# Routing inside a stream of expert products: the count product moved behind the spreading products, and turns of x placed behind routing products

## The chip, the cores and the metric

The kernel runs on one core of a Trainium2 chip. The metric is the device time of one execution in microseconds (us), as the median of several runs. The profiler takes one execution apart: PE is TensorE (its matmuls), PEld its weight loads, DVE is VectorE, ACT is ScalarE, POOL is GpSimd, SP issues DMAs.

## The reference

The input is attention with pooled keys and values, then a mixture of eight experts, each of which takes exactly 576 of 4608 tokens:

```python
def _moe_ref(x, w_gate, w1, w2):
    cap = N // E
    logits = x @ w_gate
    order = np.argsort(-logits.flatten())
    for idx in order:
        tok, e = (int(idx) // E, int(idx) % E)
        if assigned[tok] >= 0 or counts[e] >= cap:
            continue
        assigned[tok] = e
        counts[e] += 1
    ...
    for e in range(E):
        mask = assigned == e
        h = np.maximum(x[mask] @ w1[e], 0.0)
        out[mask] = h @ w2[e]
```

x has 512 columns, w1 is 512 x 1024 and w2 1024 x 512 for each expert. x is the attention's output: batch 8, 8 heads of 64, 576 positions.

## The kernel before, in words

The first 150 us are the attention, which also stores x in DRAM (`xd`) and makes the gate's logits `lg`, 128 partitions x 36 tokens x 8 experts. Then the experts run, one after the other, in the order in which they fill up. Which expert fills next and with which tokens is found by eight routing phases (`Routing.phase`). Phase 0 runs alone; phase k+1 runs in small pieces between the products of expert k.

A phase searches the threshold in four rounds. In each, DVE compares all tokens with 32 thresholds (`cmp`, L610), PE counts (nine products, L653, or L615 in phase 0), DVE picks the diagonal (`diagc`, `cnt`), PE folds (L665), DVE compares with what each expert still needs (`g`, L672), PE spreads the result to all partitions (L679), and DVE takes the maximum `up` (L681), from which the next round's places `q` come. Then `close` makes the expert's number `eid`, the running places of its tokens (PE: L713, L714), a one-hot product that puts token numbers into rows (L733, nine products), and the spreading of these to all partitions (L747, eight products). DVE turns that into `rows` (L750), with which POOL gathers the tokens' x from DRAM (`gather`, L987, five DMAs). At last DVE counts each partition's chosen tokens by expert (`per`, L759, and `pc`, L762), PE adds these over the partitions (L765), and DVE takes the sum off `need` (`left`, L767). All routing products write the one bank `rt`.

An expert has two stages. Both split f32 numbers into a high and a low part and multiply three times. Stage 1 (`stage1`, L1043) makes h = relu(x w1): 96 products of 256 columns, then 96 of 320. Stage 2 (`products`, L1077) makes 96 products of 512 columns, four rows of 24, and for the last 64 tokens 16 products at L1082. Ahead of them x must be turned: `xt` takes one piece of 128 tokens (the fifth has 64), makes four transposes into a bank `tp` (L1019; there are two such banks), ACT copies the high part `xh` and DVE the low part `xl` (L1023), which frees the bank. The weights are split in pieces by ACT (`w1h`, `w2h`) and DVE (`w1l`, L999, `w2l`, L1008), and stage 1's result by ACT (`hh`) and DVE (`hl`, L1051).

The order of everything is written at build time by the function `experts`, which keeps a clock of its own, `now`. After each main product it calls `advance`, which adds the product's expected duration and calls `step` when the expected end (`ready`) of the last routing piece on DVE has passed. `step` takes the next piece of the routing generator; a yield of two numbers tells what DVE will need until the next product may follow, and in all. `turns` places the next turn when its gather should have landed and 1.4 us have passed since the last turn; `first` and `lows` hold routing back for weights and for `xl`. `later` puts an instruction on DVE off by a given time. A routing product is thus put into PE's row at the place where its operand should be ready; if DVE is late, PE stands, as each engine works its row in order.

Of the kernel before, what the change touches and what calls it, by code (L numbers as in the profile page):

```python
# [11 lines left out]
BF = mybir.dt.bfloat16  # L12
# [3 lines left out]
OP = mybir.AluOpType  # L16
# [393 lines left out]
class Routing:  # L410
# [187 lines left out]
    def search(self, shadow, spare):  # L598
# [88 lines left out]
        self.sel = wk.tile([128, NC], BF, name="sel")  # L687
        nc.vector.tensor_scalar(self.sel, q16, up, 1.0 + EDGE, op0=OP.subtract, op1=OP.is_gt)

    def close(self, k, last):  # L690

        nc, wk, NC, lg = self.nc, self.wk, self.NC, self.lg
# [46 lines left out]
        with nc.allow_low_precision(reason="one number up to 1152 and zeros"):  # L739
            nc.vector.tensor_reduce(cp[:, 0], own, axis=AX.X, op=OP.add)  # L740
        nc.vector.tensor_scalar(cp[:, 1], cp[:, 0], 0.0, self.qcol, op0=OP.is_gt, op1=OP.mult)
        yield 0.6, 0.6
        cpv = cp.rearrange("p v (j g) -> p v j g", g=4)
        ps = self.psum()
        for g in range(4):
            for v in range(2):
                nc.tensor.matmul(ps[:, :5], self.spread[:, 96 - 32 * g:224 - 32 * g], cpv[:, v, :, g],  # L747
                                 start=(g == v == 0), stop=(g == 3 and v == 1))
        rows = wk.tile([128, 5], I32, name="rows", bufs=3)
        nc.vector.tensor_scalar(rows, ps[:, :5], -1.0, 0.0, op0=OP.add, op1=OP.max)  # L750
        self.rows = rows
# [3 lines left out]
        self.halves = halves  # L755
        yield 0.0, 0.2, "rows"

        per = wk.tile([128, NC, 8], BF, name="per")
        nc.vector.tensor_tensor(per, self.oh, sel[:, :, None].to_broadcast([128, NC, 8]), op=OP.mult)  # L759
        pc = wk.tile([128, 8], BF, name="pc")  # L760
        with nc.allow_low_precision(reason="counts up to 36"):
            nc.vector.tensor_reduce(pc, per.rearrange("p c e -> p e c"), axis=AX.X, op=OP.add)  # L762
        yield 1.15, 1.15
        ps = self.psum()
        nc.tensor.matmul(ps[:, :8], self.ones, pc, start=True, stop=True)  # L765
        left = wk.tile([128, 8], F32, name="left")
        nc.vector.tensor_tensor(left, self.need, ps[:, :8], op=OP.subtract)  # L767

        mis = wk.tile([128, 1], F32, name="mis")
        nc.vector.tensor_reduce(mis, left, axis=AX.X, op=OP.min)  # L770
# [379 lines left out]
def experts(ctx, tc, g, R, xd, w1, w2, out, ident, cap, keep):  # L1150
# [10 lines left out]

    lows = 0

    now, dve, ready = 0.0, 0.0, 0.0

    def later(after, t, f):
# [9 lines left out]

    def step(e):

        nonlocal now, ready, dve
        p, crit, t, what = held.pop() if held else next(g, (None, 0.0, 0.0, None))  # L1180
        if p is None:
            return False
        if what == "id":

            if p > e or p and pieces[p - 1].l < 8:
                held.append((p, crit, t, what))
                return False
            X.load_1(R.eid, 0, 4 if p else 2)
            eids[p] = R.eid
        elif what == "rows":  # L1190
            if p and turned[p - 1] < 5:
# [12 lines left out]
    def advance(e, t):  # L1204

        nonlocal now
        now += t
        while True:
            if waiting and waiting[0][0] <= now:
                flush(len(waiting) - 1)  # L1210
            elif ready > now or first(e) or not step(e):
                break
# [4 lines left out]
    class Pieces:  # L1217
# [10 lines left out]
        def next(self, ahead=True):  # L1228
            nonlocal dve
            if self.h == self.l:  # L1230
                self.up()
            if ahead:
                self.up()
            self.low(self.e, self.l)
            self.l += 1
            dve = max(dve, now) + 0.7
# [33 lines left out]
        elif (e, t) == (0, 4):  # L1270
            later(1.0, 0.2, lambda: X.load_2(behind(1)))

    def turns(e, upto, t0):
# [35 lines left out]
    for e in range(8):  # L1309
# [128 lines left out]
```

## Time and profile before

| | us |
|---|---|
| median of 3 runs (lowest, highest) | 624.25 (623.96, 625.15) |
| the profiled execution's own time | 624.06 |
| its span, first to last instruction | 622.2 |
| PE busy | 597.3 (96%) |
| DVE busy | 396.9 (64%) |
| ACT busy | 238.3 (38%) |

A row of the timeline gives the start, the length, the engine, line and operation, out<-in, the shape, how many of them were merged, and in brackets the idle time ahead of the first and what ended it. Matmuls overlap in these rows, as the length includes the way through the array; what one costs is the distance from its start to the next start. A row of waits gives who waited for whom, the sum, the number and the longest. A row of windows gives the stretch and its length, then the busy time and number of instructions of PE, PEld, DVE, ACT and POOL, the granted TensorE clock, the share of the DMA engines and GB/s.

### The profile page before, as it was taken

The numbers are of one execution on the slowest core, as the hardware profiler recorded it, in microseconds if no ns is written. First come the engines' busy times: TensorE is split into PE (matmuls) and PEld (weight loads), VectorE is DVE, ScalarE is ACT, GpSimd is POOL, SyncE is SP. The second block draws the span as 40 slices with busy tenths as digits, with TensorE's granted clock in tenths as the row PEclk, the third lists the DMA queues.
The fourth block names the chain that finished last, engine by engine and source line by source line (L and its number), as shares of the span: only waits on it lengthen the run. The fifth ranks groups of instructions, "written<-read, shape, count | busy, mean of one in ns | idle before, by whom it ended". The sixth has DMA issues, their size and how long they took to land.

```text
span 622.2 us, 11468 instructions
## 1 busy us (share of the span) xinstructions
PE 597.3 (96%) x4327; PEld 518.6 (83%) x4327; DVE 396.9 (64%) x1159; ACT 238.3 (38%) x554; POOL 180.1 (29%) x221
## 2 busy tenths in 40 slices
PE   8999999985999999999999999999999999999994
PEld 5999999973797789869978987897799889879972
DVE  7687777887796778858863985496378237505300
ACT  7444444451361434413532451254245225515210
POOL 2999998000200500413012302130230113020021
PEclk9999999995999999999999999999999999999997
DMA  9999961222442544319103701630190055014010
GB/s 355 419 424 410 424 219 72 76 97 85 137 145 63 200 162 135 93 52 328 29 35 130 261 1 51 238 135 18 52 330 27 34 182 207 18 52 145 2 45 36
DMA packets 32609, 92.16 MB, mean 148 GB/s; under 512 B 3473, under 2 KB 3473, under 8 KB 29857
## 3 DMA queue, kind: packets, MB, share of 16 engines
q1 hardware_dynamic: 21296, 62.92, 27.0%
q0 software_dynamic: 5920, 18.95, 9.0%
q10 hardware_dynamic: 5328, 9.48, 4.0%
q8 instruction: 35, 0.57, 0.4%
q14 instruction: 30, 0.24, 0.1%
HBM read 72.46 MB, written 18.87 MB: 147 GB/s over the span
## 4 chain that ended last, share of the span: by engine, by line
PE 83%; issue 7%; DVE 4%; DMA 2%; ACT 1%; POOL 1%; another core or an unknown queue 0%; POOLq 0%; ACTq 0%
PE h L1043 30%; PE h L1077 25%; PE psa L269 8%; PE pss L227 6%; PE h L1082 4%; PE tp L1019 2%; PE pse L256 2%; PE rt L256 1%; PE rt L653 1%; PE rt L217 1%; PE rt L615 1%; DMA rawk<-in_k_dram 1%; DMA out_dram<-yt,rows 1%; PE rt L208 1%; DMA xg<-xd,rows 1%
## 5 line engine op out<-in xcount | busy, mean ns | idle before, releaser
L1057 POOL DMA_INDIRECT out_dram<-yt,rows x29 | 31.4, 1082 | 247.0 <-ACT yt L1091 246.6
L1077 PE MATMUL h<-w2h,hh 128*128 128x512 f32 x256 | 102.5, 400 | 0.3 <-PEq L1141 0.3
L1077 PE MATMUL h<-w2l,hh 128*128 128x512 f32 x256 | 101.9, 398 | 0.0
L1077 PE MATMUL h<-w2h,hl 128*128 128x512 f32 x256 | 101.0, 395 | 0.0
L1043 PE MATMUL h<-xh,w1l 128*128 128x320 f32 (+1 forms) x512 | 95.4, 301 | 0.0
L1048 ACT ACTIVATE hh<-h 128x320 fp32r<-128x320 f32 (+1 forms) x128 | 52.4, 410 | 108.6 <-PE h L1043 102.6
L1043 PE MATMUL h<-xl,w1h 128*128 128x320 f32 (+1 forms) x512 | 92.8, 300 | 0.0
L1043 PE MATMUL h<-xh,w1h 128*128 128x320 f32 (+1 forms) x512 | 91.8, 300 | 0.3 <-ACT xh L1021 0.3
L987 POOL DMA_INDIRECT xg<-xd,rows x40 | 42.3, 1056 | 131.8 <-DVE rows L750 48.6
L1043 PEld LDWEIGHTS h<-xh,w1h 128*128 128x128 f32 x512 | 75.3, 190 | 3.5 <-issue 2.7
L1043 PEld LDWEIGHTS h<-xh,w1l 128*128 128x128 f32 x512 | 77.2, 189 | 0.5
L1043 PEld LDWEIGHTS h<-xl,w1h 128*128 128x128 f32 x512 | 76.2, 190 | 0.0
L1023 DVE TENSOR_TENSOR xl<-tp,xh 128x512 fp32r<-128x512 f32 (+1 forms) x40 | 25.3, 633 | 70.8 <-ACT xh L1021 70.1
L1051 DVE SCALAR_TENSOR_TENSOR hl<-h,hh 128x320 fp32r<-128x320 f32 (+1 forms) x128 | 56.7, 451 | 20.9 <-ACT hr L1050 16.0
L1091 ACT ACTIVATE yt<-h 128x512 f32<-128x512 f32 x32 | 19.1, 598 | 127.5 <-PE h L1077 83.6
L269 PE MATMUL psa<-vblk,eT 128*128 128x146 f32 (+3 forms) x400 | 62.1, 302 | 0.0
L1077 PEld LDWEIGHTS h<-w2l,hh 128*128 128x128 f32 x256 | 48.2, 188 | 8.9
L1077 PEld LDWEIGHTS h<-w2h,hh 128*128 128x128 f32 x256 | 48.4, 189 | 8.6 <-issue 0.7
L1077 PEld LDWEIGHTS h<-w2h,hl 128*128 128x128 f32 x256 | 48.2, 188 | 8.5
L269 PEld LDWEIGHTS psa<-vblk,eT 128*128 128x128 f32 (+1 forms) x400 | 52.2, 180 | 1.7 <-issue 0.3
L999 DVE TENSOR_TENSOR w1l<-raw,w1h 128x512 fp32r<-128x512 f32 x64 | 41.9, 687 | 13.0 <-ACT w1h L995 13.0
L1008 DVE TENSOR_TENSOR w2l<-raw,w2h 128x512 fp32r<-128x512 f32 x64 | 43.2, 681 | 3.4 <-ACT w2h L1005 3.4
(216 smaller groups left out, 898.8 us busy)
## 6 DMA issues: line engine op xcount, KB each, us to landing
raw<-in_moe_w_dram SPq DMA_DIRECT2D x64, 512.0 KB, 6.5
xd<-xt ACTq DMA_DIRECT2D x36, 256.0 KB, 4.4
rawv<-in_v_dram SPq DMA_DIRECT2D x7, 1280.0 KB, 14.0
rawk<-in_k_dram SPq DMA_DIRECT2D x7, 1152.0 KB, 13.8
rawq<-in_q_dram SPq DMA_DIRECT2D x7, 1152.0 KB, 12.2
rawk<-in_k_dram SPq DMA_DIRECT2D x2, 576.0 KB, 4.6
rawv<-in_v_dram SPq DMA_DIRECT2D x1, 768.0 KB, 7.8
rawq<-in_q_dram SPq DMA_DIRECT2D x1, 640.0 KB, 8.9
```

Source lines behind the costliest of these rows:

```text
L227: nc.tensor.matmul(ps[cols, j // 2, 144 * (j % 2):144 * (j % 2) + 144], self.q_of(b, j, n, cols.stop - cols.start), self.kblk[b % 4][:, j] ...
L269: self.nc.tensor.matmul(o[h], self.eT[i][:, c, h], self.vblk[b % 4][:, self.BLOCKS[c]:self.BLOCKS[c + 1]], start=(c == cs[0]), stop=(c == ...
L987: nc.gpsimd.indirect_dma_start(out=self.xg[:n, t, :], out_offset=None, in_=self.xd, in_offset=bass.IndirectOffsetOnAxis(ap=rows[:n, t:t + ...
L999: self.nc.vector.tensor_tensor(l, raw, h.bitcast(F32), op=OP.subtract)
L1008: self.nc.vector.tensor_tensor(self.w2l[:, i], self.raw2[e][:, i], self.w2h[:, i].bitcast(F32), op=OP.subtract)
L1023: later(1.3, 0.65, lambda: nc.vector.tensor_tensor(xl, ps[:, :, :n], xh, op=OP.subtract))
L1043: nc.tensor.matmul(ps[:, :m], a[:, j, fs], b[:, j, o], start=(n == 0), stop=(n == 11))
L1048: nc.scalar.activation(hh[:, f, o], ps[:, :m], AF.Relu)
L1051: later(0.65, 0.4, lambda f=f, o=o, m=m, ps=ps: nc.vector.scalar_tensor_tensor(hl[:, f, o], ps[:, :m], 0.0, hh[:, f, o].bitcast(F32), op0= ...
L1057: st = nc.gpsimd.indirect_dma_start(out=rows, out_offset=bass.IndirectOffsetOnAxis(ap=idx, axis=0), in_=y, in_offset=None)
L1077: nc.tensor.matmul(ps, a[:, f, o], b[:, f], start=(f == 0 and k == 0), stop=(f == 7 and k == 2))
L1082: nc.tensor.matmul(ps[64 * a:64 * a + 64, :256], self.hr[:, f], self.raw2[e][:, f, 256 * a:256 * a + 256], start=(f == 0), stop=(f == 7))
```

## The change

Three things are done. First, in all phases but 0 the counts of a partition (`per`, `pc`) are made on DVE ahead of the spreading products, right behind `cp`, and the product that adds them over the partitions follows directly behind the eight spreading products, into columns 8 to 15 of the same bank. The planner is told that DVE needs 1.75 us there, not 0.6. Second, `step` notes with `fresh` that it has just put a routing product into PE's row, and `turns` places a turn only then, or when the routing has ended (`through`), or when the turn is overdue (`t < late`). In stage 1 `turns` is now called behind `advance`, so that the turn stands directly behind the product. Third, the earliest place of a turn in stage 1 of experts 1 to 7 is no longer fixed at the tenth product.

```diff
@@ close @@
         nc.vector.tensor_scalar(cp[:, 1], cp[:, 0], 0.0, self.qcol, op0=OP.is_gt, op1=OP.mult)
-        yield 0.6, 0.6
+        if k:
+            pc = self.chosen(sel)
+        yield (1.75, 1.75) if k else (0.6, 0.6)
...
                 nc.tensor.matmul(ps[:, :5], self.spread[:, 96 - 32 * g:224 - 32 * g], cpv[:, v, :, g],
                                  start=(g == v == 0), stop=(g == 3 and v == 1))
+        if k:
+            nc.tensor.matmul(ps[:, 8:16], self.ones, pc, start=True, stop=True)
...
-        per = wk.tile([128, NC, 8], BF, name="per")
-        nc.vector.tensor_tensor(per, self.oh, sel[:, :, None].to_broadcast([128, NC, 8]), op=OP.mult)
-        pc = wk.tile([128, 8], BF, name="pc")
-        with nc.allow_low_precision(reason="counts up to 36"):
-            nc.vector.tensor_reduce(pc, per.rearrange("p c e -> p e c"), axis=AX.X, op=OP.add)
-        yield 1.15, 1.15
-        ps = self.psum()
-        nc.tensor.matmul(ps[:, :8], self.ones, pc, start=True, stop=True)
+        if not k:
+            pc = self.chosen(sel)
+            yield 1.15, 1.15
+            ps = self.psum()
+            nc.tensor.matmul(ps[:, 8:16], self.ones, pc, start=True, stop=True)
         left = wk.tile([128, 8], F32, name="left")
-        nc.vector.tensor_tensor(left, self.need, ps[:, :8], op=OP.subtract)
+        nc.vector.tensor_tensor(left, self.need, ps[:, 8:16], op=OP.subtract)
@@ experts: step @@
-        p, crit, t, what = held.pop() if held else next(g, (None, 0.0, 0.0, None))
+        if held:
+            p, crit, t, what = held.pop()
+        else:
+            p, crit, t, what = next(g, (None, 0.0, 0.0, None))
+            fresh, coming, through = fresh or coming, crit > 0, p is None
@@ experts: advance @@
         now += t
+        fresh = False
@@ experts: turns @@
-        if t < upto and due(e, "rows", 6.5 + 1.3 * t) and now >= last + 1.4:
+        if t < upto and due(e, "rows", 6.5 + 1.3 * t) and now >= last + 1.4 and (fresh or through or t < late):
@@ experts: stage 1, stage 2 @@
-            if (10 if e else 2) <= n < 96:
-                turns(e, 5, n)
+            if not e and 2 <= n < 96:
+                turns(e, 5, 5)
...
             advance(min(e + 1, 7), dt)
+            if e and n < 96:
+                turns(e, 5, 3 + (n - 14) // 24)
...
-                turns(e + 1, 3, n)
+                turns(e + 1, 3, (n - 52) // 12)
```

`chosen` holds the five removed lines that make `per` and `pc`, and returns `pc`. Line numbers behind it grow by 10 to 11: L747 becomes L759, L765 becomes L762 (L776 in phase 0), L1019 becomes L1030, L1043 becomes L1054, L1077 becomes L1088.

What this does to the rows of instructions is shown at three places. The first is PE in stage 1 of expert 2, where the last of the eight spreading products (`spread`) and the count product (`pc`) stand. Before:

```order
L747 LDWEIGHTS spread
L747 MATMUL rt<-cp,spread 128x5
L1043 MATMUL h<-xh,w1l 128x256
L1043 MATMUL h<-xl,w1h 128x256 x4
L1043 MATMUL h<-xh,w1h 128x256 x4
L1043 MATMUL h<-xh,w1l 128x256 x4
L1043 MATMUL h<-xl,w1h 128x256 x4
L765 LDWEIGHTS ones
L765 MATMUL rt<-pc,ones 128x8
L1043 MATMUL h<-xh,w1h 128x256 x4
```

Now:

```order
L759 LDWEIGHTS spread
L759 MATMUL rt<-cp,spread 128x5
L762 LDWEIGHTS ones
L762 MATMUL rt<-pc,ones 128x8
L1054 MATMUL h<-xh,w1l 128x256 x3
```

The 17 main products between the two are gone; the same holds in the other phases from 1 to 7. The stretch from the last of L733's nine products to the first of L747's eight grew from 13 main products to 21 in experts 2 to 6, from 17 to 25 in expert 1 and from 5 to 10 in expert 0.

The second place is PE in the same stage, at the products that make the running places (`untri`, `tri`) and at the fourth and fifth turn (`tp`). Before:

```order
L1019 MATMUL tp<-ident,xg 128x64 x4
L1043 MATMUL h<-xh,w1l 128x256
L1043 MATMUL h<-xl,w1h 128x256 x4
L1043 MATMUL h<-xh,w1h 128x256 x4
L1043 MATMUL h<-xh,w1l 128x256
L713 LDWEIGHTS untri
L713 MATMUL rt<-ones,untri 128x1
L714 LDWEIGHTS tri
L714 MATMUL rt<-inc,tri 128x1
L1043 MATMUL h<-xh,w1l 128x256 x3
```

Now:

```order
L1054 MATMUL h<-xl,w1h 128x256 x3
L723 LDWEIGHTS untri
L723 MATMUL rt<-ones,untri 128x1
L724 LDWEIGHTS tri
L724 MATMUL rt<-inc,tri 128x1
L1030 MATMUL tp<-ident,xg 128x128 x4
L1054 MATMUL h<-xl,w1h 128x256
```

The fourth turn stands directly behind `tri` now; the fifth, of 64 tokens, stands directly behind L743's nine products (L733 before). So it is in experts 2 to 6. In expert 1 these two stand behind the products of L679 and L653. In stage 2 of experts 1 to 4 all three turns stand directly behind a product of L653, L665 or L679, where before they stood together between main products. That makes 24 turns behind a routing product. In stage 2 of expert 5 the three turns stood behind the 1st, 6th and 11th product and stand behind the 65th, 77th and 89th now; in expert 6 they keep their places. The turns of expert 0 are not behind routing products.

The third place is DVE in stage 1 of expert 1, between two comparisons with `need` (`g`), at the fourth round's `cmp`. Before:

```order
L672 TENSOR_TENSOR g_247<-rt,need_2764 32x8
L1008 TENSOR_TENSOR w2l<-raw_2900,w2h 128x512
L681 TENSOR_REDUCE up<-rt 128x1
L684 TENSOR_SCALAR q_3091<-q32c,up 128x36
L610 TENSOR_TENSOR cmp<-q_3091,j_196 128x1152
```

Now:

```order
L672 TENSOR_TENSOR g_247<-rt,need_2762 32x8
L1062 SCALAR_TENSOR_TENSOR hl<-h,hh 128x256
L681 TENSOR_REDUCE up<-rt 128x1
L684 TENSOR_SCALAR q_3076<-q32c,up 128x36
L610 TENSOR_TENSOR cmp<-q_3076,j_196 128x1152
L641 SCALAR_TENSOR_TENSOR lo<-steps,up,lo 128x1
L646 SCALAR_TENSOR_TENSOR hi<-steps,lo 128x1
L1062 SCALAR_TENSOR_TENSOR hl<-h,hh 128x256
L657 TENSOR_TENSOR diagc<-rt,dq 128x32
L661 TENSOR_REDUCE cnt<-diagc 128x8
L1019 TENSOR_TENSOR w2l<-raw_2899,w2h 128x512
```

The `w2l` that stood between `g` and `up` stands behind `cnt` now, and an `hl` stands in its place. In stage 2 of experts 1 to 4 an `xl` of a turn, and one or two `w1l`, stand between a `g` and the next `up`, where before nothing did.

More of the change, by code (lines that the diff above doesn't have):

```diff
@@ L688, in search, with chosen @@
         nc.vector.tensor_scalar(self.sel, q16, up, 1.0 + EDGE, op0=OP.subtract, op1=OP.is_gt)
+    def chosen(self, sel):
+        nc, wk, NC = self.nc, self.wk, self.NC
+        per = wk.tile([128, NC, 8], BF, name="per")
+        nc.vector.tensor_tensor(per, self.oh, sel[:, :, None].to_broadcast([128, NC, 8]), op=OP.mult)
+        pc = wk.tile([128, 8], BF, name="pc")
+        with nc.allow_low_precision(reason="counts up to 36"):
+            nc.vector.tensor_reduce(pc, per.rearrange("p c e -> p e c"), axis=AX.X, op=OP.add)
+        return pc
     def close(self, k, last):
@@ L1162, in experts @@
     lows = 0
+    fresh, coming, through = False, False, False
     now, dve, ready = 0.0, 0.0, 0.0
@@ L1177, in step @@
     def step(e):
-        nonlocal now, ready, dve
-        p, crit, t, what = held.pop() if held else next(g, (None, 0.0, 0.0, None))
+        nonlocal now, ready, dve, fresh, coming, through
+        if held:
[3 more added lines that the diff above has]
+            fresh, coming, through = fresh or coming, crit > 0, p is None
         if p is None:
@@ L1204, in advance @@
     def advance(e, t):
-        nonlocal now
+        nonlocal now, fresh
         now += t
+        fresh = False
         while True:
@@ L1271, in turn, with turns @@
             later(1.0, 0.2, lambda: X.load_2(behind(1)))
-    def turns(e, upto, t0):
+    def turns(e, upto, late):
         nonlocal last
         t = turned.get(e, 5)
-        if t < upto and due(e, "rows", 6.5 + 1.3 * t) and now >= last + 1.4:
+        if t < upto and due(e, "rows", 6.5 + 1.3 * t) and now >= last + 1.4 and (fresh or through or t < late):
             last = now
```

## The prediction

> **What bounds the kernel now.** I read the busy rows first, then the span cut at the experts' stages, then the chain of waits, and last PE's timeline at the places that the change touches. Names: a *main* product is one of L1043 (stage 1), L1077 or L1082 (stage 2); a *routing* product is one of L653, L665, L679, L713, L714, L733, L747, L765; a *turn* is the four transposes of L1019.
>
> ```profile
> PE 597.3 (96%) x4327; PEld 518.6 (83%) x4327; DVE 396.9 (64%) x1159; ACT 238.3 (38%) x554; POOL 180.1 (29%) x221
> 220.00:250.00 30.00, 29.41 (x254) 28.19 (x253) 24.37 (x78) 12.67 (x35) 2.79 (x3) 1.00 0.43 146
> 308.00:336.00 28.00, 28.00 (x171) 21.12 (x171) 15.09 (x48) 8.80 (x17) 4.99 (x8) 1.00 0.10 38
> PE rt L653 <- DVE cmp L610: 0.6, 1, 0.6
> PEld tp L1019 <- DVE xl L1023: 1.2, 3, 0.5
> ```
>
> In the windows the first figure behind the length is PE's busy time: 28.00 of 28.00 us in the second; the first, expert 1, lacks 0.59, which is the wait of L653 for DVE. So in the experts' part the end is set by PE, by the sum of the steps between its instructions. A microsecond comes out of the kernel only if a step on PE gets shorter or a wait there disappears; work that moves on DVE, ACT or POOL costs nothing as long as PE doesn't stand.
>
> **What a small product costs between main ones.** A busy PE hides this, so I read starts, not durations.
>
> ```profile
> 207.22 0.39 PE L1077 MATMUL h<-w2l,hh 128*128 128x512 f32 x1
> 207.45 0.18 PE L765 MATMUL rt<-pc,ones 128*128 128x8 bf16 x1
> 207.49 0.48 PE L1077 MATMUL h<-w2h,hh 128*128 128x512 f32 x1
> 207.81 0.39 PE L1077 MATMUL h<-w2h,hl 128*128 128x512 f32 x1
> 208.03 0.39 PE L1077 MATMUL h<-w2l,hh 128*128 128x512 f32 x1
> 208.26 0.39 PE L1077 MATMUL h<-w2h,hh 128*128 128x512 f32 x1
> 208.49 0.60 PE L1019 MATMUL tp<-ident,xg 128*128 128x128 f32 x4
> 208.84 0.48 PE L1077 MATMUL h<-w2h,hl 128*128 128x512 f32 x1
> 209.16 0.39 PE L1077 MATMUL h<-w2l,hh 128*128 128x512 f32 x1
> ```
>
> Main products follow each other by 0.23 us (207.81, 208.03, 208.26). Around the lone L765 the steps are 0.23, 0.04 and 0.32, so it costs 0.04 of its own and 0.09 on the main product behind it, 0.13 together. The turn costs 0.35 (208.49 to 208.84) and again 0.09 behind it, 0.44 together. The weight loads tell what the 0.09 is:
>
> ```profile
> 207.45 0.20 PEld L1077 LDWEIGHTS h<-w2h,hh 128*128 128x128 f32 x1
> 207.57 0.19 PEld L1077 LDWEIGHTS h<-w2h,hl 128*128 128x128 f32 x1
> 208.82 0.19 PEld L1077 LDWEIGHTS h<-w2h,hl 128*128 128x128 f32 x1
> 208.93 0.19 PEld L1077 LDWEIGHTS h<-w2l,hh 128*128 128x128 f32 x1
> ```
>
> Two f32 loads that nothing separates start 0.11 to 0.12 apart (207.45 and 207.57, 208.82 and 208.93). Behind a long product such a load runs in that product's 0.23 us; behind a product of 0.04 it lies open. The four transposes pay three open loads among themselves (0.35 is 3 x 0.11 and 0.03) and one on the main product behind.
>
> **The change part by part. 1: the count product.** It leaves its place of its own in seven of eight phases and becomes the ninth product behind the eight of L747.
>
> ```profile
> 291.04 0.64 PE L1043 MATMUL h<-xl,w1h 128*128 128x256 f32 x4
> 291.52 0.18 PE L765 MATMUL rt<-pc,ones 128*128 128x8 bf16 x1
> 291.56 0.72 PE L1043 MATMUL h<-xh,w1h 128*128 128x256 f32 x4
> 232.43 0.40 PE L1043 MATMUL h<-xh,w1l 128*128 128x256 f32 x2
> 233.43 0.39 PE L653 MATMUL rt<-oh,cmp 128*128 128x32 bf16 x9 [0.59 <-DVE cmp L610]
> 233.66 0.48 PE L1043 MATMUL h<-xh,w1l 128*128 128x256 f32 x2
> ```
>
> In stage 1 the lone product costs 0.04 and the 0.08 by which four main products got longer (0.72 for 0.64): 0.12. One more in a row costs 0.23 / 9 = 0.03 (233.43 to 233.66). Of the seven, two stood in stage 2 and five in stage 1: 2 x (0.13 - 0.03) + 5 x (0.12 - 0.03) = 0.65 us less. I take it whole.
>
> What it adds: the two DVE instructions of the counts now stand ahead of the spreading products, whose row waits for them. Their price is 289.86 to 290.35 + 0.67, 1.16 us:
>
> ```profile
> 287.88 0.23 DVE L736 TENSOR_TENSOR rowd<-rt,dq 128x80 f32<-128x80 f32 x1
> 288.42 0.23 DVE L741 TENSOR_SCALAR cp<-cp,qcol 128x20 f16<-128x20 f16 x1
> 289.86 0.45 DVE L759 TENSOR_TENSOR per<-oh,sel 128x288 bf16<-128x288 bf16 x1
> 290.35 0.67 DVE L762 TENSOR_REDUCE pc<-per 128x8 bf16<-128x288 bf16 x1
> ```
>
> With L736 to L741 (287.88 to 288.65, 0.77) DVE needs 1.9 us between L733's products and L747's. In experts 2 to 6 the order puts 21 main products (0.12 each, 2.5 us) and the 64-row turn (0.58, below) there where 13 stood: 3.1 us. Ahead of those DVE instructions stand up to two `hl` or `xl` (0.33 and 0.60), 0.9 at most; 2.8 against 3.1 still fits. It is tighter in expert 0, ten products of 0.23, 2.3 us. Without this cover each phase would stand by what is missing. Behind L747 wait `rows`, which now needs the ninth product too (0.03), and the gather on POOL; the turns that read it come 26 main products of 0.23 behind, as before, or many more, so its 1.5 us of delay is free.
>
> **2: the wait of expert 1 goes.** At 232.43 two main products start, 0.12 each, so the next step was due at 232.67; L653 started at 233.43: 0.76 us lost. Its cause on DVE:
>
> ```profile
> 231.53 0.69 DVE L1008 TENSOR_TENSOR w2l<-raw,w2h 128x512 fp32r<-128x512 f32 x1 [1.35 <-ACT w2h L1005]
> 232.14 0.16 DVE L681 TENSOR_REDUCE up<-rt 128x1 f32<-128x8 f32 x1
> 232.61 0.76 DVE L610 TENSOR_TENSOR cmp<-q,j 128x1152 bf16<-128x1152 f16 x1
> ```
>
> `w2l` stood in DVE's row ahead of `up` and waited 1.35 us for ACT, and `up`, `q` and `cmp` came late with it. In the new order that `w2l` stands behind the count of this comparison (shown with the change), an `hl` ahead of `up` instead. From `up` to `cmp`'s end (233.37) are 1.23 us and 0.06 more to the product; the 14 main products of 0.12 that the order puts there give 1.7, and an `hl` of 0.33 in the way still fits. So the wait goes whole: 0.76. What is late next is `w2l`, by some 2 us; stage 2, its reader, is about a hundred main products off.
>
> **3: the third turn of expert 5's stage 2.**
>
> ```profile
> 481.15 0.39 PE L1077 MATMUL h<-w2h,hl 128*128 128x512 f32 x1
> 481.60 0.66 PE L1019 MATMUL tp<-ident,xg 128*128 128x128 f32 x4
> 482.01 0.48 PE L1077 MATMUL h<-w2l,hh 128*128 128x512 f32 x1
> 480.86 0.69 DVE L1023 TENSOR_TENSOR xl<-tp,xh 128x512 fp32r<-128x512 f32 x1
> ```
>
> The steps are 0.45 and 0.41 where 0.23 and 0.35 are usual: 0.28 lost, because the first turn's bank is free only when `xl` (to 481.55) has read it. The three turns now stand behind products 65, 77 and 89, 2.7 us apart, not 1.6, so this 0.28 goes. In expert 6 the turns keep their places and the same wait.
>
> **4: 24 turns behind a routing product.** No turn of before follows a routing product closely on a running PE, so this is bounded. Above: 0.09, if the turn and the product shared the one open load behind them. Below: 0.00; the turn's first load, which now hides in a main product, would lie open behind a tiny one, and the main product behind the turn still pays its own. By the loads 0.11 apart I am near the lower end: 0.01 for each of the 18 turns of 128 rows, 0.2 us. The six of 64 rows differ:
>
> ```profile
> 281.94 0.52 PE L1043 MATMUL h<-xh,w1l 128*128 128x256 f32 x3
> 282.39 0.46 PE L1019 MATMUL tp<-ident,xg 64*128 64x64 f32 x4
> 282.78 0.38 PE L1043 MATMUL h<-xh,w1l 128*128 128x256 f32 x1
> 283.00 0.51 PE L1043 MATMUL h<-xl,w1h 128*128 128x256 f32 x3
> 282.39 0.32 PEld L1019 LDWEIGHTS tp<-ident,xg 64*128 64x128 f32 x4
> ```
>
> From the last of three (281.94 and two steps of 0.12, 282.18) to the second product behind (283.00) are 0.82, less two usual steps 0.58. Its load starts with it at 282.39, not a product earlier, so 0.21 pass where 0.12 are usual: here the load is open already, and behind a routing product it is paid once for both. Half of 0.09 each, as the tail of the product still has to run out: 6 x 0.05 = 0.3 us.
>
> The Trainium skill ("TensorE: Matmul & The Clock Gate", section "LDWEIGHTS (loading the stationary operand)") gives a load as its columns / 1.2 in ns whatever the rows, 107 ns for 128 columns; the 0.11 of these rows agree. By that rule each turn owes its loads whoever stands ahead of it, part 4 is nothing, and the sum would be 1.7 us. It holds for 64 rows too, and there this trace differs: four loads in 0.32 with 0.14 for the last one leave 0.06 each.
>
> **Sum.** 0.65 + 0.76 + 0.28 + 0.2 + 0.3 = 2.2 us. The profiled execution took 624.06 with a span of 622.2; it becomes 621.9. The median shown is 624.25, 0.2 above it, so I predict 622.0.
>
> **The rivals.** *Turns share the load:* all 24 gain 0.09, 2.2 us instead of 0.5, 620.4. For it: the 0.09 appears behind every group of small products alike, whatever its length. Against: the loads 0.11 apart in a turn. Chance 0.17.
>
> *Turns share nothing:* part 4 is zero, 622.5. For it, the same rows read strictly. Chance 0.20.
>
> *Waits move rather than go.* In experts 2 to 4 the second comparison now has an `xl`, and `w1l` ahead of it, in DVE's row between `g` and `up`. PE leaves a turn and nine products, 0.44 + 9 x 0.23 = 2.5 us; DVE needs up to 0.6 + 0.6 + 1.23, 2.4. If they come 0.3 late, 0.9 in three places, or if the wait of part 2 returns elsewhere, the gain is 1.3 or less: 623.1. Chance 0.13.
>
> *Slower:* a turn behind a routing product puts its `xl`, which waits for ACT, ahead of the next routing step on DVE. Twelve turns in the second stages of experts 1 to 4 stand so, and eight of them ahead of a step that PE waits for (`up` or the diagonal sum). If ACT is late as it was for `w2l` (1.35 above), `xl` and all behind it are late too; where 0.45 of that outlasts the products between, eight places make 3.6 us against 2.2 gained: 625.5. It decides from 0.28 us a place on. Against it: ACT is a third busy in these windows (8.80 of 28.00), and PE has 2 us of main products between such steps. Chance 0.06.
>
> **How the numbers follow.** My own case has 0.44. The range reaches from the sharing of loads, 620.4, to the moved waits, 623.1; a little is put to both sides for the median of another measurement: 620.3 to 623.2. About 0.2% (1.25 us, from 623.0) is what a measurement tells from no change. Faster by more: my case, both cases on the turns, and a little of the moved waits, 0.82. Within: the rest of these, 0.12. Slower: 0.06.
>
> **What would show it.** Right: in the profile after, the windows of experts 1 to 6 are full for PE; no wait of L653 for L610; no row of the count product alone between main ones; steps of 0.03 from L747's last to it. A turn behind L665 or L679 takes 0.43 more than the routing product alone (with sharing 0.35), and the 64-row turn behind L733 0.53. Wrong: new PE waits for `cmp`, `g` or `pc`, above all where an `xl` stands ahead of `up`; or a step from L747 to the count product that is longer than 0.03, which says that `pc` is late.

## The result, and the profile after

| | before | after |
|---|---|---|
| median of the runs made beside each other | 624.7 (623.96 to 625.8, 4 runs) | 621.43 (621.3 to 621.63, 4 runs) |
| the profiled execution's own time | 624.06 | 621.30 |
| its span | 622.2 | 619.5 |

The ratio of the times is 0.994 (95% interval 0.9927 to 0.9952). The forecast was 622.0 in a range from 620.3 to 623.2, and faster.

Windows of before and of the kernel after; the columns are those of the windows in the prediction, with PE's busy time first. Before, expert 0's second stage:

```profile
190.00:220.00 30.00, 30.00 (x188) 22.45 (x187) 20.80 (x70) 8.74 (x18) 9.90 (x13) 1.00 0.44 145
```

After, the same stretch, expert 1's first stage and expert 2's second:

```profile
190.00:220.00 30.00, 29.68 (x185) 22.18 (x183) 20.51 (x69) 8.61 (x17) 9.73 (x13) 1.00 0.45 145
220.00:250.00 30.00, 30.00 (x259) 28.96 (x258) 25.88 (x90) 13.64 (x37) 3.30 (x3) 1.00 0.44 149
308.00:336.00 28.00, 28.00 (x168) 21.15 (x167) 12.80 (x41) 8.25 (x16) 4.95 (x9) 1.00 0.10 39
```

Expert 1 (220 to 250) is full now; it lacked 0.59. But the window ahead of it, expert 0's second stage, lacks 0.32, and was full.

PE's timeline of the kernel after, at a turn behind L665, at a 64-row turn behind L743 and at the count product L762 behind L759:

```profile
312.06 0.39 PE L1088 MATMUL h<-w2l,hh 128*128 128x512 f32 x1
312.29 0.18 PE L665 MATMUL rt<-cnt,fold 128*128 128x8 f16 x1
312.33 0.64 PE L1030 MATMUL tp<-ident,xg 128*128 128x128 f32 x4
312.72 0.48 PE L1088 MATMUL h<-w2h,hh 128*128 128x512 f32 x1
313.04 0.40 PE L1088 MATMUL h<-w2h,hl 128*128 128x512 f32 x1
...
283.90 0.64 PE L1054 MATMUL h<-xh,w1l 128*128 128x256 f32 x4
284.38 0.51 PE L743 MATMUL rt<-OHb,OHa 128*128 128x80 f16 x9
284.83 0.46 PE L1030 MATMUL tp<-ident,xg 64*128 64x64 f32 x4
285.22 0.74 PE L1054 MATMUL h<-xl,w1h 128*128 128x256 f32 x4
285.79 0.40 PE L1054 MATMUL h<-xh,w1h 128*128 128x256 f32 x2
...
287.82 0.36 PE L759 MATMUL rt<-cp,spread 128*128 128x5 f16 x8
288.05 0.17 PE L762 MATMUL rt<-pc,ones 128*128 128x8 bf16 x1
```

From 312.06 to 313.04 are 0.98 us; two usual steps are 0.45, so L665 and the turn cost 0.52 together. Apart they cost 0.13 and 0.445. All turns of 128 rows that follow a routing product read so, by 0.045 to 0.060 us each. From 283.90 to 285.79 are 1.89, less eight usual steps of 0.12 about 0.93: that is L743 with the 64-row turn (0.936 on unrounded start times). Apart the two cost 0.425 and 0.583.

The wait that was new in this execution, on PE, with ACT and DVE ahead of it:

```profile
217.64 0.39 PE L653 MATMUL rt<-oh,cmp 128*128 128x32 bf16 x9 [0.32 <-DVE cmp L610]
```

```profile
210.96 0.60 PE L1030 MATMUL tp<-ident,xg 128*128 128x128 f32 x4
```

```profile
213.49 0.60 ACT L1032 ACTIVATE xh<-tp 128x512 fp32r<-128x512 f32 x1 [2.38 <-PE tp L1030]
```

```profile
214.12 0.69 DVE L1034 TENSOR_TENSOR xl<-tp,xh 128x512 fp32r<-128x512 f32 x1 [2.16 <-ACT xh L1032]
216.83 0.75 DVE L610 TENSOR_TENSOR cmp<-q16a,j 128x1152 bf16<-128x1152 f16 x1
```

The turn that starts at 210.96 ends at 211.56, but ACT, idle for 2.38 us, takes it only at 213.49. DVE's `xl`, the rest of its row and `cmp` come late with it, and PE stands. PE had finished, ACT was free: the release between them came 1.9 us late. In experts 2 to 6 of this execution two products of PE each are taken late in the same way, by 0.3 to 2.2 us, but nothing waits there in the end. (The 22 places that the expectations below speak of are counted by PE's update records; some of these are only missing from the trace, with ACT on time.)

### The profile page after: what moved, and what is told of

Same layout as the page of the kernel before. It is cut to its first block, busy times and chain, and to the rows that moved or that the text cites. A ratio compares the mean times of both kernels' runs of the same rounds, so it can differ in the third digit from the quotient of the medians.

```text
span 619.5 us, 11472 instructions
## 1 busy us (share of the span) xinstructions
PE 596.0 (96%) x4327; PEld 519.0 (84%) x4327; DVE 395.3 (64%) x1159; ACT 238.0 (38%) x554; POOL 177.8 (29%) x221
## 4 chain that ended last, share of the span: by engine, by line
PE 81%; issue 7%; DVE 4%; DMA 3%; POOL 2%; SPq 0%; ACT 0%; POOLq 0%; another core or an unknown queue 0%; ACTq 0%
PE h L1054 30%; PE h L1088 25%; PE psa L269 7%; PE pss L227 5%; PE h L1093 4%; PE tp L1030 3%; DMA rawk<-in_k_dram 2%; PE pse L256 2%; PE rt L256 1%; PE rt L653 1%; PE rt L217 1%; DMA out_dram<-yt,rows 1%; PE rt L615 1%; DVE xl L1034 1%; PE rt L208 1%
## 5 line engine op out<-in xcount | busy, mean ns | idle before, releaser
L1088 PE MATMUL h<-w2h,hh 128*128 128x512 f32 x256 | 101.5, 396 | 0.3 <-PEq L1152 0.3
L1088 PE MATMUL h<-w2h,hl 128*128 128x512 f32 x256 | 101.5, 397 | 0.0
L1088 PE MATMUL h<-w2l,hh 128*128 128x512 f32 x256 | 101.0, 394 | 0.0
L1054 PE MATMUL h<-xl,w1h 128*128 128x320 f32 (+1 forms) x512 | 94.2, 301 | 0.0
L1054 PE MATMUL h<-xh,w1h 128*128 128x320 f32 (+1 forms) x512 | 91.5, 299 | 0.3 <-issue 0.3
L1054 PE MATMUL h<-xh,w1l 128*128 128x320 f32 (+1 forms) x512 | 91.6, 298 | 0.0
L1054 PEld LDWEIGHTS h<-xh,w1h 128*128 128x128 f32 x512 | 75.4, 189 | 3.5 <-issue 3.4
L1054 PEld LDWEIGHTS h<-xl,w1h 128*128 128x128 f32 x512 | 76.1, 190 | 0.4
L1054 PEld LDWEIGHTS h<-xh,w1l 128*128 128x128 f32 x512 | 75.9, 189 | 0.1
L998 POOL DMA_INDIRECT xg<-xd,rows x40 | 40.0, 1001 | 124.0 <-DVE halves L768 67.5
L1088 PEld LDWEIGHTS h<-w2h,hh 128*128 128x128 f32 x256 | 48.2, 188 | 9.5 <-issue 0.7
L1088 PEld LDWEIGHTS h<-w2l,hh 128*128 128x128 f32 x256 | 48.2, 188 | 9.1
L1088 PEld LDWEIGHTS h<-w2h,hl 128*128 128x128 f32 x256 | 48.3, 189 | 8.6
L1019 DVE TENSOR_TENSOR w2l<-raw,w2h 128x512 fp32r<-128x512 f32 x64 | 43.1, 680 | 3.0 <-ACT w2h L1016 2.8
```

Of the source, the lines that this page charges most:

```text
L998: nc.gpsimd.indirect_dma_start(out=self.xg[:n, t, :], out_offset=None, in_=self.xd, in_offset=bass.IndirectOffsetOnAxis(ap=rows[:n, t:t + ...
L1019: self.nc.vector.tensor_tensor(self.w2l[:, i], self.raw2[e][:, i], self.w2h[:, i].bitcast(F32), op=OP.subtract)
L1054: nc.tensor.matmul(ps[:, :m], a[:, j, fs], b[:, j, o], start=(n == 0), stop=(n == 11))
L1088: nc.tensor.matmul(ps, a[:, f, o], b[:, f], start=(f == 0 and k == 0), stop=(f == 7 and k == 2))
```

## The experiments

The profiled executions differ by up to 2 us in when the experts begin, which the change does not touch. So beside the median each kernel has its *stretch*, from the first main product of expert 0 to the last of expert 7, as these two rows of before, at 161.05 and 609.03, mark it:

```profile
161.05 0.73 PE L1043 MATMUL h<-xh,w1h 128*128 128x256 f32 x4 [0.26 <-ACT xh L1021]
609.03 0.39 PE L1077 MATMUL h<-w2l,hh 128*128 128x512 f32 x1
```

Each ratio is to runs of the kernel before that were made beside that kernel's own.

| kernel | begins | stretch, us | median (runs) | ratio to before, 95% |
|---|---|---|---|---|
| before | 161.05 | 447.98 | | |
| after | 160.94 | 445.33 | 621.43 (4) | 0.9927 to 0.9952 |
| after, once more | 162.75 | 444.97 | 621.06 (5) | 0.9933 to 0.9959 |
| counts alone | 161.31 | 446.20 | 622.75 (9) | 0.9970 to 0.9989 |
| turns alone | 161.32 | 445.23 | 621.63 (6) | 0.9948 to 0.9972 |
| turns one product apart | 161.01 | 446.76 | 622.78 (12) | 0.9973 to 0.9990 |
| count first | 160.86 | 444.99 | 621.37 (6) | 0.9947 to 0.9975 |
| count first, turns spaced | 160.90 | 444.67 | 621.23 (6) | 0.9940 to 0.9968 |
| the same, with pairs of turns | 161.12 | 444.75 | 621.09 (4) | 0.9935 to 0.9968 |
| count first, no cover | 161.25 | 451.33 | 627.48 (4) | 1.0034 to 1.0067 |

Where no disturbance is seen the stretch repeats to about 0.15: it is 444.97 and 444.99 for two orders of the same products, and 445.12 for the kernel with added rows below, which is the kernel after up to its end. Those 0.15 are the first L665 of expert 0, whose wait for DVE differs from one execution to the next: it cost 0.23 in both executions of after and 0.38 there. A group's cost below is its length by start times less the usual steps of its main products.

### The counts alone

```diff
-        yield 0.6, 0.6
+        if k:
+            pc = self.chosen(sel)
+        yield (1.75, 1.75) if k else (0.6, 0.6)
+            nc.tensor.matmul(ps[:, 8:16], self.ones, pc, start=True, stop=True)
```

(with the turns by the old rule)

> The kernel before with the first part of the change alone: in phases 1 to 7 the count product stands directly behind the eight spreading products, and the turns are placed by the old rule. By the steps of the changed kernel's trace (the nine together cost 0.33, the eight alone 0.30 and the lone count product 0.12) this alone is worth 0.70 us, so the profiled execution should be 624.06 - 0.7 = 623.4, less or more what the old waits of 0.76 and 0.28 do in this order. On the late releases that I saw in the changed kernel (ACT stands idle 1 to 2 us for a product of PE that ended long before, 22 times, each time within 8 us behind a spreading row): if two products that both release a waiter and end 0.03 us apart are the cause, this kernel shows them too, behind all seven spreading rows; if the new places of the turns are the cause, it shows none, as the kernel before shows none.

The stretch is 1.78 us shorter than before. The seven spreading rows and count products cost 2.31 us together where they cost 2.13 and 0.86: 0.68 less. Expert 1's wait for `cmp` is gone too (0.74), though the turns stand by the old rule, so either part of the change moves `w2l` out of the way. About half of the remaining 0.36 is routing products that came to stand elsewhere around the changes from stage 2 to stage 1: an L665 cost 0.21 at the end of expert 0's stage 2 and costs 0.12 behind the change, and an L679 that stands right at expert 1's change costs 0.1 more there but takes up 0.2 by which two steps of the change were longer without it. The rest is spread over smaller differences. There was no late release in this execution, so the pair of releasing products does not make them every time.

### The turns alone

The second and third part of the change, with `close` as before.

> The changed kernel with the count product put back to its own place and its own time (the second and third part of the change alone). If a turn directly behind a routing product saves about 0.05 us with 128 rows and 0.07 to 0.09 with 64 rows, as the steps of the changed kernel read, 24 turns are worth 1.4 us, and with the wait of expert 1 (0.76) and that of expert 5 (0.28) gone the profiled execution is 624.06 - 2.4 = 621.7. If, as I predicted, they are worth 0.5, it is 622.5; if nothing, 623.0. On the late releases: none if the pair of the last spreading product and the count product makes them, some if the turns do.

2.75 us shorter: 0.74 and 0.28 for the two waits, some 1.4 for the turns, and about 0.3 that is again mostly at changes of stage. No late release here either. Alone, this part does as much as both in the first profiled execution of after, since it has no late releases. The counts' 1.78 adds to it only in small part: expert 1's wait goes once, and the 0.3 of each kernel is not there in the order of both (3.01 in the repeated profile).

### The turns one product apart

```diff
         now += t
-        fresh = False
+        stale, fresh = fresh, False
...
-... and (fresh or through or t < late):
+... and (stale or through or t < late):
```

> The changed kernel with one edit: a turn goes behind the first main product after a routing product, not directly behind the routing product. All turns and routing products otherwise keep their places to within a product or two. If it is being adjacent that pays, the turns cost 0.448 each again (0.58 with 64 rows) in place of 0.39 (0.49 to 0.51), and the time rises by 18 x 0.05 + 6 x 0.075 = 1.4 us to 622.7. If the gain came from where the turns stand (waits, DVE's order) and not from adjacency, the time stays at 621.3; by the prediction's own sizes (0.01 and 0.05) it rises by 0.5 to 621.8.

PE's timeline of this kernel, at the same place as above:

```profile
312.48 0.39 PE L1088 MATMUL h<-w2l,hh 128*128 128x512 f32 x1
312.71 0.18 PE L665 MATMUL rt<-cnt,fold 128*128 128x8 f16 x1
312.75 0.48 PE L1088 MATMUL h<-w2h,hh 128*128 128x512 f32 x1
313.06 0.60 PE L1030 MATMUL tp<-ident,xg 128*128 128x128 f32 x4
313.41 0.48 PE L1088 MATMUL h<-w2h,hl 128*128 128x512 f32 x1
313.73 0.39 PE L1088 MATMUL h<-w2l,hh 128*128 128x512 f32 x1
```

From 312.48 to 313.73 are 1.25, less three steps 0.57, where the adjacent pair costs 0.52. Against the undisturbed kernel with the count first the stretch is 1.77 us longer. Summed over the 24 groups, it is 0.87 for the 18 turns of 128 rows (0.049 each) and 0.45 for the six of 64 rows (0.075 each): 1.33 by adjacency alone. Another 0.3 is the first L665 of expert 0, whose wait for DVE is longer in this execution (0.51 against 0.19), and some hundredths lie on the main products around. So being adjacent pays, not the place.

### The count product first

```diff
+        if k:
+            nc.tensor.matmul(ps[:, 8:16], self.ones, pc, start=True, stop=True)
         for g in range(4):
             for v in range(2):
                 nc.tensor.matmul(ps[:, :5], ...)
-        if k:
-            nc.tensor.matmul(ps[:, 8:16], self.ones, pc, start=True, stop=True)
```

> The changed kernel with the count product ahead of the eight spreading products instead of behind them. Nine products cost the same 0.33, and the subtraction behind needs no release of its own, so PE never has two releasing products 0.03 us apart. If that pair is what makes PE's releases late, there are no releases later than 0.15 us in this trace, the wait of expert 0's comparison (0.39 us at 217.6 in the changed kernel, behind an x piece that ACT got 1.9 us late) is gone, and the time is 621.3 - 0.4 = 620.9. If the late releases have another cause, they are still there behind the seven spreading rows and the time stays 621.3.

The late releases and the wait are gone, and the profiled execution took 620.85. That is what the theory of the pair expected; the repetition of after shows that it proves nothing.

### After, once more

> The changed kernel itself once more, since neither the kernel with the counts alone nor the one with the turns apart, which both have the pair of releasing products, showed a late release. If the late releases belong to the kernel, this profile has some twenty of them again, and the wait of 0.4 us for cmp at the end of expert 0. If they were an accident of that one execution, it has none, and from the first main product of expert 0 to the last of expert 7 it takes 445.0 us as with the count product ahead, not 445.33.

ACT's timeline in this execution, at the first two of the same three turns of expert 0's second stage (PE starts these two at 211.18 and 212.78):

```profile
211.81 0.60 ACT L1032 ACTIVATE xh<-tp 128x512 fp32r<-128x512 f32 x1 [1.15 <-PE tp L1030]
212.31 0.62 ACT L1006 ACTIVATE w1h<-raw 128x512 fp32r<-128x512 f32 x1
213.41 0.60 ACT L1032 ACTIVATE xh<-tp 128x512 fp32r<-128x512 f32 x1 [0.48 <-PE tp L1030]
```

The second `xh` starts 0.63 us after its turn starts, not 2.53. No release is late, no L653 waits, and the stretch is 444.97. The same program thus had the late releases in one execution and not in another. The theory of the pair fell altogether with the next kernels: two without the pair (no cover, and turns in pairs) showed late releases at the same places again.

### Turns apart where no routing is left

```diff
-... and now >= last + 1.4 and ...
+... and now >= last + (2.5 if through else 1.4) and ...
```

> The kernel with the count product ahead of the spreading products, and the turns of expert 6's second stage, where no routing is left, 2.5 us apart instead of 1.4. The third of them stood 0.28 us for a bank (0.73 where 0.45 is usual). From the first main product of expert 0 to the last of expert 7 it should take 444.7 us in place of 445.0, and the median 621.1; if the turn waits for something else, 445.0.

PE's timeline at the third turn of expert 6's second stage, in the first profile of after and then in this kernel:

```profile
533.19 0.39 PE L1088 MATMUL h<-w2h,hl 128*128 128x512 f32 x1
533.64 0.66 PE L1030 MATMUL tp<-ident,xg 128*128 128x128 f32 x4
534.06 0.48 PE L1088 MATMUL h<-w2l,hh 128*128 128x512 f32 x1
```

```profile
535.05 0.39 PE L1088 MATMUL h<-w2l,hh 128*128 128x512 f32 x1
535.28 0.60 PE L1030 MATMUL tp<-ident,xg 128*128 128x128 f32 x4
535.63 0.48 PE L1088 MATMUL h<-w2h,hh 128*128 128x512 f32 x1
```

The steps 0.45 and 0.42 became 0.23 and 0.35; the stretch is 0.3 us shorter than that of the repeated after and the shortest of all. The medians (621.23 and 621.06) cannot tell this from nothing.

### The disputed cost by itself

Rows of products on PE behind the kernel's end; `main` is an f32 product with a new weight each time, `small` a bf16 product of 8 columns.

```diff
+    for c in (512, 256, 128, 64):
+        for i in range(16):
+            main(i, c)
+    for t in (0, 4):
+        for i in range(4):
+            turn(4, t)
+    for group in (lambda: small(), lambda: small(9), lambda: turn(1), lambda: turn(2), lambda: turn(4),
+                  lambda: (small(), turn(4)), lambda: (small(9), turn(4)),
...
+                  lambda: (turn(4), turn(4))):
+        for i in range(8):
+            group()
+            for k in range(5):
+                main(i + k)
```

> The changed kernel with rows of products on PE added behind its end, whose result nobody reads: main products of 512, 256, 128 and 64 columns with a new weight each, turns without anything between, and small groups between five main products of 512 columns. My theory now: an f32 load of a main product takes 0.12 us when nothing covers it, that of a transpose 0.06, and the 0.11 between transposes is the time in which 128 columns pass. So main products go down to a step of 0.12 us and stay there at 128 and 64 columns (by the rival, that columns alone count, 0.06 and 0.03); transposes of 128 rows follow each other by 0.11, of 64 rows by 0.06; one transpose between main products costs 0.12 us, two 0.23, four 0.446; a small product alone 0.13, with a turn behind it 0.52 and not 0.58, nine with a turn 0.72 and not 0.78; two turns behind each other 0.83 to 0.88. By the rule of my prediction (the transposes' pitch is open loads, nothing is shared) the small product with a turn costs 0.57.

Main products followed each other by 0.227 us with 512 columns, 0.120 with 256, 0.111 with 128 and 0.111 with 64: a load that nothing covers takes 0.111, as the theory has it. The steps between starts in the groups, to the second main product behind, as means of the eight groups of a kind:

| group | steps, us |
|---|---|
| small, main, main | 0.039, 0.314 |
| turn, main, main | 0.108, 0.110, 0.109, 0.028, 0.316 |
| small, turn, main, main | 0.039, 0.143, 0.109, 0.109, 0.029, 0.318 |
| one transpose, main, main | 0.026, 0.313 |
| two turns, main, main | seven of 0.108 to 0.109, 0.028, 0.319 |

PE of this kernel, its first such group, and its loads (PEld):

```profile
679.68 0.18 PE L1170 MATMUL h<-ones 128*128 128x8 bf16 x1
679.72 0.64 PE L1175 MATMUL h<-ident,xg 128*128 128x128 f32 x4
680.11 1.41 PE L1166 MATMUL h<-w2h,hh 128*128 128x512 f32 x5
```

```profile
679.68 0.10 PEld L1170 LDWEIGHTS <-ones 128*128 128x128 bf16 x1 [0.27 <-issue]
679.70 0.42 PEld L1175 LDWEIGHTS h<-ident,xg 128*128 128x128 f32 x4
680.09 0.54 PEld L1166 LDWEIGHTS h<-w2h,hh 128*128 128x128 f32 x3
```

Behind a small product a main product comes 0.314 - 0.227 = 0.087 late; a transpose comes 0.143 - 0.108 = 0.035 late. The difference, 0.052, is what a turn behind a routing product saves. The four loads of the turn take 0.42, not 0.47 (three steps of 0.11 and 0.14 for the last): the second, which nothing holds up, starts 0.06 behind the first, the others only when a transpose has gone on.

The groups with 64-row turns, with the step ahead of them counted in, cost 0.59 for the turn alone, 0.62 with one small product ahead and 0.81 with nine, where the sums of the parts are 0.73 and 0.92. So with 64 rows 0.11 is shared. Part of it is seen in the step of the main product ahead: 0.32 ahead of the lone 64-row turn, 0.23 ahead of the small product that stands before such a turn.

One expectation failed in its letter: the row of transposes without anything between went 0.213 us apart, not 0.11. The windows of this kernel show why:

```profile
616.00:619.20 3.20, 3.20 (x31) 3.20 (x30) 0.00 (x0) 0.00 (x0) 0.00 (x0) 1.00 0.00 0
619.20:622.60 3.40, 3.40 (x18) 3.28 (x17) 0.00 (x0) 0.00 (x0) 0.00 (x0) 0.50 0.00 0
622.60:623.90 1.30, 1.30 (x18) 1.08 (x17) 0.00 (x0) 0.00 (x0) 0.00 (x0) 0.99 0.00 0
```

The clock granted was 0.50 for 3.4 us, and 0.213 is twice 0.107. The transposes of 64 rows behind them, at 0.99, went 0.062 apart. So the pitch in a turn goes with the clock and falls with the columns that pass, and with 128 rows its loads, 0.06 apart where nothing holds them, are not what it shows. With 64 rows 0.062 is near both, half of 0.109 and the loads' 0.06; no run parts the two.

### No cover for the counts

```diff
-        yield (1.75, 1.75) if k else (0.6, 0.6)
+        yield 0.6, 1.75 if k else 0.6
```

> The kernel with the count product ahead of the spreading products, but the planner is told that DVE needs 0.6 us there, as before the change, not 1.75. Nothing else is edited. The row of spreading products then stands behind 11 main products of 0.12 us in experts 2 to 6, not 21, and behind 5 of 0.23 in expert 0, not 10. With the cover, DVE has pc 0.58 us before its product starts (286.69 against 287.27) in experts 2 to 6, 0.34 in expert 0 and 1.23 in expert 1. Without it PE should stand 10 x 0.12 - 0.58 = 0.62 us in each of experts 2 to 6, 5 x 0.23 - 0.34 = 0.8 in expert 0 and nothing in expert 1, 3.9 us in all: 445.0 + 3.9 = 448.9 us from the first main product of expert 0 to the last of expert 7, and a time of 625, above the kernel before. If the merge were free without the cover, as the rival has it, 445.0.

PE's waits from 190 to 560 us, and its timeline at the spreading row of expert 0:

```profile
PE rt L758 <- DVE pc L697: 3.3, 6, 0.7
PE rt L653 <- DVE cmp L610: 1.2, 2, 0.6
```

```profile
203.08 0.18 PE L758 MATMUL rt<-pc,ones 128*128 128x8 bf16 x1 [0.69 <-DVE pc L697]
```

The kernel is 0.5% slower than before. The seven rows cost 4.5 us more than with the cover (0.85 in expert 0, 0.65 to 0.68 in each of experts 2 to 6, 0.25 in expert 1), where 3.9 was expected. The other 1.9 I had not counted: two comparisons wait, 0.7 each. One of them is the wait that the change had removed, back in expert 1. DVE and PE of this kernel there:

```profile
231.41 0.15 DVE L672 TENSOR_TENSOR g<-rt,need 32x8 bf16<-32x8 f32 x1 [0.26 <-PE rt L665]
232.79 0.69 DVE L1019 TENSOR_TENSOR w2l<-raw,w2h 128x512 fp32r<-128x512 f32 x1 [1.22 <-ACT w2h L1016]
233.40 0.16 DVE L681 TENSOR_REDUCE up<-rt 128x1 f32<-128x8 f32 x1
233.87 0.76 DVE L610 TENSOR_TENSOR cmp<-q,j 128x1152 bf16<-128x1152 f16 x1
```

```profile
234.69 0.39 PE L653 MATMUL rt<-oh,cmp 128*128 128x32 bf16 x9 [0.59 <-DVE cmp L610]
```

`w2l` stands between `g` and `up` again, waits for ACT, and `cmp` is late by the same 0.59 as before the change. The other is expert 0's, behind a late release, so its 0.7 is not the missing cover's. Three more comparisons, in experts 2, 3 and 4, lost about 0.2 each.

### Turns in pairs

The kernel with the turns spaced, where a lone turn takes the next one directly behind it.

```diff
+            alone = not fresh
             turn(e, t)
+            if alone and t in (0, 3) and t + 1 < upto and due(...):
+                turn(e, t + 1)
```

> The kernel with the count first and the turns of expert 6 apart, and now the first two of the three turns that stand alone in the second stages of experts 5 and 6, and the two in the first stage of expert 7, directly behind each other. If any f32 transpose behind a short product saves 0.05 us, as in the added rows, where two turns cost 0.89 and one 0.46, this saves 3 x 0.04 = 0.1 us and the stretch from the first main product of expert 0 to the last of expert 7 takes 444.55 us in place of 444.68. If the second turn waits for its bank or for x, it is more than 444.68. The median can't tell 0.1 us from nothing.

The 0.1 did not come: 444.75 against 444.67. The eight transposes cost 0.89 in experts 5 and 6, a lone turn 0.445. The added rows had said so already, had I read their steps and not their sums: the step from turn to turn is 0.109, and a lone turn ends with 0.028 and 0.09 on the main product behind, 0.12. There is nothing to share.

## Why the prediction was right, step by step

The order of the sum is that of the prediction, against the first profiled execution after (2.76 us, of which 2.65 in the stretch).

| term | predicted | measured |
|---|---|---|
| 1 count product | 0.65 | 0.68 |
| 2 wait of expert 1 | 0.76 | 0.74 |
| 3 third turn of expert 5 | 0.28 | 0.28 |
| 4 eighteen turns of 128 rows | 0.2 | 0.9 |
| 4 six turns of 64 rows | 0.3 | 0.45 |
| late releases of that execution | none | -0.36 to -0.39 |

**What bounds the kernel** held: every gain and loss found lies in PE's steps and waits.

**Step 1** held in both halves. The ninth product in the row costs 0.02 us (0.328 for the nine in experts 2 to 6, 0.305 for the eight before), not more. And the DVE instructions ahead of it were covered: their operand is there 0.58 us early in experts 2 to 6 and 0.34 in expert 0, the place called tighter (read in the kernel with the count first). That this zero had a price was shown by taking the cover away.

**Step 2** held, with its cause: the kernel without cover puts `w2l` ahead of `up` and gets the wait back. What did not follow is that it needs this change; either half of it moves `w2l`.

**Step 3** held (0.732 to 0.445 for that turn), and expert 6's third turn kept its wait, as said.

**Step 4** is where the prediction failed. Its sentence "By the loads 0.11 apart I am near the lower end: 0.01" took the pitch of the transposes for their open loads, and so the load ahead of the first for 0.11 as well. The pitch is the passing of 128 columns; the transpose comes 0.035 late behind a small product, where a main product comes 0.087 late. With 0.05 for 0.01 the 18 turns are worth 0.9. For the 64-row turns the bounds held (expert 1's gain of 0.09 is at the upper one): the sharing was 0.075 on the average and not half of 0.09. The sum of terms 1 to 4 would have been 3.05, and an undisturbed execution gives 3.01 in the stretch.

The rule that was weighed there (the Trainium skill, "TensorE: Matmul & The Clock Gate", section "LDWEIGHTS (loading the stationary operand)") gives 107 ns for 128 columns whatever the rows. The added rows bear it out for f32 main products (0.111 at 128 and 64 moving columns). For the loads of transposes, 0.06 apart where nothing holds them, they do not.

**The rivals.** Sharing in full (0.09 a turn) and sharing nothing were both wrong; the truth stood between, a little nearer to the first. No wait moved into experts 2 to 4: their windows are full. The slower case named the right chain at last, an `xl` that waits for ACT ahead of a routing step, but for a wrong reason and in one place, with a turn of expert 0 that stands behind no routing product: ACT was not late by its own work but got its release late, and it cost 0.39 us once. That the time came out as near as it did is partly this accident, which took back some of what step 4 had missed.

What would show it: the full windows, the steps of 0.03 and the missing wait of expert 1 came as written; "0.43 more than the routing product alone" was 0.39, and 0.53 for the 64-row turn was 0.51. One sign of being right did not come, and one of being wrong did: in the first profiled execution L653 waits for `cmp` at 217.64, in expert 0. That wait came with a late release and not with the order on DVE, which the signs were meant for; in the repeated profile no L653 waits.

## What to carry to other kernels

Read what a short product leaves open from the step of the instruction behind it, for each kind of follower: the same 0.04 us product cost 0.087 in front of a main product and 0.035 in front of a transpose. A steady pitch does not tell whether loads or passing columns set it; the second load behind a short product does. And an edit costed at nothing because it is covered should be priced without the cover: here that was 4.5 us at the place itself, and more again by the order that came with it.

## What the runs showed of the hardware that was not expected

**Releases of PE that come late.** In three of the ten profiled executions of the kernel after and its variants (after, pairs of turns, no cover), ACT took one to four products of PE in each of experts 2 to 6 late, by 0.3 to 2.7 us from the product's end (some of these because the instruction ahead of them on ACT was late), and in two of them (after, no cover) a turn of expert 0, which cost PE time. The same program showed them once and once not. ACT and POOL of the first execution after, in expert 2's first stage:

```profile
293.08 0.39 ACT L1059 ACTIVATE hh<-h 128x256 fp32r<-128x256 f32 x1 [1.04 <-PE h L1054]
296.06 0.44 ACT L1059 ACTIVATE hh<-h 128x320 fp32r<-128x320 f32 x1 [2.07 <-PE h L1054]
```

```profile
288.70 0.98 POOL L998 DMA_INDIRECT xg<-xd,rows  x1 [7.71 <-DVE halves L768]
293.85 0.92 POOL L998 DMA_INDIRECT xg<-xd,rows  x1 [0.30 <-issue]
```

The products that these two read had ended at 292.02 and 293.78. The late ones lie within or just behind the gather's five issues, the first of them, at 288.70, and the last shown here; the three executions agree in the places to within a product or two. The pair of releasing products is not needed, since two kernels without it show them. The new places of the turns are not enough, since the same program shows them once and once not; whether they are needed is not shown, as only two profiles, before and counts alone, have the old places. What the cause is stays open, and so does whether executions without a profiler have it; the medians cannot tell 0.4 us.

**The clock fell though PE's busy row shows no idle time**: to 0.50 for 3.4 us behind 32 main products of 128 and 64 columns, at the first of the transposes. The Trainium skill ("TensorE: Matmul & The Clock Gate", section "Part 1: The HAM clock gate (the "warmup" mystery)") gives a window of 3413 ns, at half the clock after an idle one; the length agrees with this trace, but PE's busy row was full throughout the window before (3.20 of 3.20 us). That row does not tell how much of a step the columns take: by the 0.227 for 512 columns, 64 would pass in 0.03 of the 0.111. Whether that counts as idle for the clock was not tried.
